# A fused attention and feed-forward kernel: q and k of the first four pairs loaded in longer packets and turned by TensorE

## The chip, the cores and the metric

The kernel runs on one core of one Trainium2 chip. The metric is the device time of one execution in microseconds (us). The core has five engines with their own instruction queues, which run in order and wait for one another on semaphores: TensorE (PE, with its weight loads shown apart as PEld), VectorE (DVE), ScalarE (ACT), GpSimd (POOL) and SyncE (SP). Sixteen DMA engines move data; SP, ACT and POOL issue the transfers. TensorE writes only PSUM, from which ACT and DVE copy.

## The reference, cut to what matters

```python
batch, n_heads, seq, head_dim = 8, 8, 576, 64
scores = scale * np.matmul(q, k.transpose(0, 1, 3, 2))
thresh = np.max(scores, axis=-1, keepdims=True) - tau
scores = np.where(scores >= thresh, scores, -1000000000.0)
scores = scores - np.max(scores, axis=-1, keepdims=True)
attn = np.exp(scores)
attn = attn / (np.sum(attn, axis=-1, keepdims=True) + 1e-09)
attn_out = np.matmul(attn, v)
x = attn_out.transpose(0, 2, 1, 3).reshape(B * S, H * D)      # 4608 x 512
h = x @ w_in                                                  # 512 x 2048, float64 input
g = h * (1.0 / (1.0 + np.exp(-1.702 * h)))
out = g @ w_out                                               # 2048 x 512, float64 input
```

The attention inputs are fp32. The two weight matrices come as 64-bit floats, and the kernel turns them into fp32 itself with integer and float steps on ACT and DVE.

## The kernel before

**Pairs.** The 64 heads are worked as 32 pairs of heads (pair n is two heads of batch n // 4). One pair goes through these steps, and each is a function in the code:

- `load_qk` (L392): q and k of one head, each as two DMAs of 32 columns. A packet is 32 floats, 128 bytes. A pair's q, or its k, is 2304 packets. The data lands in 32x32 blocks, ready for the next step.
- `prep` (L501): one DVE transpose of 32x32 blocks (L504) turns 128x576 of q, another those of k, so that the head dimension lies on the partitions.
- `scores` (L510, L514): for each of nine key blocks j, four matmuls of 64 partitions fill one PSUM tile of the pool psA (three tiles of two banks).
- `keep` (L527, L531): ACT copies that tile to SBUF.
- `in_groups` (L533, L537), `over_tiles`, `over_halves`: DVE reduces to the row maximum. For most pairs `turn_rows`, `row_out` (L630) and `row_in` (L639) send the maximum to DRAM and back, spread over the partitions; POOL issues that for pairs 0 to 7. Pair 2 spreads it on DVE instead (`spread_max`, L618).
- `sub` (L645, DVE), `mask` (L651, ACT) and `exps` (L655, ACT), five tiles a pair.
- `values` and `sums_by_pe` (L666): products with v, and with ones for the sums. For pairs 0 to 4 the sums are made on TensorE; later pairs reduce on DVE.
- `one_row` (L697), `spread_sums` (L749, L751), `place_x` (L768): DVE divides and writes x for the dense layers.

**Weights.** Each of 32 pieces of 512 KB is loaded by SP (`load_w`, L453) and converted in steps: `cv_power` (L461) and `cv_power2` (L465) on ACT, `cv_low` (L472) on DVE, `cv_round` on ACT for w_in (L479) or `cv_whole` on DVE for w_out (L486), and `cv_end` (L493) on DVE.

**Dense layers.** The first two blocks of 256 rows of x go through `mm1_0` (L823), `tanh`, `gelu_0` (L829) and `mm2` (L805) once pairs 0 to 3 are placed. Later blocks use seven products where eight would be needed (L783, L974 and, near the end, L888), with sums of weights that are made once by ACT, and by DMAs that add (L930, L934). `gelu` is L795.

**Order.** No engine picks work at run time. While the program is built, a planner (`run_in_order`) plays the tasks through, each with an engine, an estimated cost, a rank, the tasks it follows and the buffers it takes and gives back; of what is ready, an engine takes the lowest rank. Its choices become the fixed order of each queue. The rank of a pair's task is the pair's number plus a bias by function, from the tables `EARLY` (pairs 0 to 3), `SECOND` (4 to 7) and `LATER`; weight steps have `CV` and `W_RANK`. Loads of a pair have rank n - 2 plus the bias, v's own. Pairs 1 and 3 (`APART`) keep their raw, turned and score tiles in a second arena; the other pairs share one set of raw and turned tiles, so a load waits until its predecessor was turned.

```python
    def two_loads(n, which, cost, r, queue, behind, take):
        ys, a = [], None
        ring = RING[1] if queue is nc.sync else ()
        for h in range(2):
            a = task(
                "SP", cost, r, load_qk, n, which, queue, h,
                after=behind + ([a] if h else []), take=ring if h else tuple(take) + ring,
            )
```

Of the kernel before, what the change touches and what calls it, by code (L numbers as in the profile page):

```python
# [21 lines left out]
P = 128  # L22
# [10 lines left out]
def kernel(  # L33
# [84 lines left out]
    minus = const.tile([P, 2, KT], FP32, name="minus")  # L118
    own_row = const.tile([P, QB // 2], FP32, name="own_row")
# [10 lines left out]
    for x in ("raw0", "raw1", "qkT0", "qkT1", "mb"):  # L130
# [6 lines left out]
        "exps": 11.43,  # L137
        "in_groups": -31.63,
        "keep": -11.23,
        "load_qk": 20.14,  # L140
        "load_v": 19.9,
        "mask": 171.06,
        "one_row": -45.66,
        "over_halves": -1.59,
        "over_tiles": -20.68,
        "place_x": -28.05,
        "prep": -4.32,
        "row_in": 9.72,
        "row_out": -14.48,
        "scores_run": -28.58,  # L150
        "spread_max": 3.58,
        "spread_sums": 14.71,
        "sub": 178.85,
        "sums_by_pe": 312.21,
        "turn_rows": -14.38,
        "values": -19.56,
        "w_sum": -20.0,
    }
    SECOND = {
        "exps": 6.76,  # L160
        "in_groups": 291.18,
        "keep": 29.15,
        "load_qk": 165.77,
        "load_v": 335.03,
        "mask": 337.17,
        "one_row": -25.48,
        "over_halves": -20.33,
        "over_tiles": 311.35,
        "place_x": 0.09,
        "prep": -16.41,  # L170
        "row_in": 205.66,
        "row_out": 181.09,
        "scores_run": 21.47,
        "spread_sums": -6.66,
        "sub": 17.25,
        "sums_by_pe": 334.76,
        "sums_in": -21.09,
        "sums_out": 5.24,
        "turn_rows": 184.92,
        "turn_sums": -18.91,  # L180
        "values": -19.14,
    }
    LATER = {
        "exps": 208.23,
        "in_groups": 342.52,
        "keep": -7.99,
        "load_qk": 197.24,
        "load_v": -11.46,
        "mask": 344.07,
        "over_halves": -19.6,  # L190
        "over_tiles": 19.84,
        "place_x": 181.51,
        "prep": 208.92,
        "row_in": -6.54,
        "row_out": -30.86,
        "scores_run": -0.21,
        "sub": 200.03,
        "sums_in": 338.15,
        "sums_out": 7.27,
        "turn_rows": 167.17,  # L200
        "turn_sums": 343.8,
        "values": -25.3,
        "x_sum": -9.1,
# [1281 lines left out]
```

## Time and profile before

| | us |
|---|---|
| three runs: median (lowest to highest) | 1299.56 (1298.23 to 1299.97) |
| the profiled execution: its time | 1299.66 |
| its span | 1297.9 |
| PE busy | 1252.3 |
| DVE busy | 986.2 |
| ACT busy | 677.7 |
| first scores (L514) start | 9.06 |
| scores of pair 1 start | 21.41 |
| `mm1_0` (L823) starts | 108.59 |

The profile is one execution. The span runs from the first to the last instruction, and the execution's own time is 1.8 us longer. A row of the timeline gives the start, the duration, the engine, the line, what is written and read, the count, and in brackets the idle time of the engine just before and what ended it. Matmul counts of the profile are records: an fp32 matmul leaves two. The granted clock is the clock that TensorE was given, 1.00 being full.

### The profile page before, as it was taken

How to read it: one execution, taken by the hardware profiler on the slowest of the kernel's cores; microseconds unless marked ns; L12 is line 12 of the kernel's file. 1: busy time of each engine (PE TensorE's matmuls, PEld its weight loads, DVE VectorE, ACT ScalarE, POOL GpSimd, SP SyncE). 2: the span in 40 equal slices, each digit the busy share in tenths (PEclk: the TensorE clock that was granted, in tenths of full speed). 3: DMA queues.
4: the chain of work that ended last, by engine and by line, in shares of the span. 5: the costliest groups of instructions: out<-in, count | busy, mean ns of one | idle time of the engine just before them, and what ended most of it. 6: DMA issues, size and time to landing. Idle time of an engine off the chain costs nothing. (4 is left out here: it accounts for less than half of the span.)

```text
span 1297.9 us, 22745 instructions
## 1 busy us (share of the span) xinstructions
PE 1252.3 (96%) x9128; PEld 972.9 (75%) x9128; DVE 986.2 (76%) x1553; ACT 677.7 (52%) x878; POOL 240.6 (19%) x277
## 2 busy tenths in 40 slices
PE   4689999999999999999999999999999999999998
PEld 2347854577777888777777788887777788888887
DVE  6999987989988787777887878777778863652642
ACT  5999876686755545454555555544546540210210
POOL 1000101131030303021120312030302117120120
PEclk8799999999999999999999999999999999999999
DMA  9735356183222222222122222222221100000000
GB/s 243 179 76 146 109 132 115 58 144 84 72 55 56 56 72 56 72 47 64 55 48 63 47 63 56 72 56 73 55 61 35 51 27 17 1 1 33 1 1 33
DMA packets 190825, 87.01 MB, mean 67 GB/s; under 512 B 159872, under 2 KB 170112, under 8 KB 190720
## 3 DMA queue, kind: packets, MB, share of 16 engines
q1 hardware_dynamic: 182560, 78.08, 23.7%
q0 software_dynamic: 5792, 7.19, 3.1%
q8 instruction: 71, 1.16, 0.4%
q10 hardware_dynamic: 2368, 0.30, 0.2%
q14 instruction: 34, 0.28, 0.1%
HBM read 71.63 MB, written 9.70 MB: 63 GB/s over the span
## 5 line engine op out<-in xcount | busy, mean ns | idle before, releaser
L537 DVE TRANSPOSE_TENSOR_REDUCE part<-arena 128x36 f32<-128x1152 f32 (+1 forms) x295 | 358.1, 1236 | 48.1 <-ACT arena L531 38.2
L783 PE MATMUL hps<-xT,w_in 128*128 128x256 f32 x1536 | 338.9, 381 | 2.9 <-DVE arena L795 2.9
L783 PEld LDWEIGHTS hps<-xT,w_in 128*128 128x128 f32 x1536 | 291.8, 191 | 48.9 <-issue 5.3
L651 ACT ACTIVATE arena<-arena 128x1152 f32<-128x1152 f32 (+1 forms) x160 | 169.4, 1059 | 127.4 <-DVE arena L645 127.2
L531 ACT COPY arena<-ps 128x576 f32<-128x576 f32 x288 | 171.0, 642 | 111.8 <-PE ps L514 108.9
L645 DVE TENSOR_TENSOR arena<-arena 128x1152 f32<-128x1152 f32 (+1 forms) x158 | 202.1, 1320 | 19.2 <-DMA arena<-row 19.1
L974 PE MATMUL ops<-w_out,arena 128*128 128x256 f32 x896 | 202.7, 381 | 1.7 <-DVE arena L795 1.6
L655 ACT ACTIVATE arena<-arena,shift,scl 128x1152 f32<-128x1152 f32 (+1 forms) x160 | 200.1, 1250 | 4.0
L974 PEld LDWEIGHTS ops<-w_out,arena 128*128 128x128 f32 x896 | 169.1, 190 | 29.4 <-DVE arena L795 3.8
L514 PE MATMUL ps<-arena 64*64 64x288 f32 x2304 | 172.1, 413 | 19.5 <-DVE neg L1035 9.1
L940 POOL TENSOR_TENSOR arena<-arena 128x256 f32<-128x256 f32 x56 | 51.8, 925 | 647.1 <-DVE arena L795 544.0
L666 PE MATMUL pv<-arena 64*64 64x288 f32 x2176 | 159.6, 407 | 0.0
L974 PE MATMUL ops<-arena 128*128 128x256 f32 x672 | 150.6, 380 | 0.0
L792 ACT ACTIVATE th<-hps 128x512 f32<-128x512 f32 x112 | 66.1, 590 | 161.7 <-PE hps L783 148.2
L514 PEld LDWEIGHTS ps<-arena 64*64 64x64 f32 x2304 | 85.4, 135 | 81.5 <-ACT arena L531 17.5
L974 PEld LDWEIGHTS ops<-arena 128*128 128x128 f32 x672 | 127.3, 190 | 19.3 <-issue 2.2
L666 PEld LDWEIGHTS pv<-arena 64*64 64x64 f32 x2176 | 81.0, 133 | 54.7 <-issue 8.8
L996 DVE SCALAR_TENSOR_TENSOR osb<-ops,osb 128x256 f32<-128x256 f32 x98 | 39.6, 415 | 94.2 <-PE ops L974 88.0
L795 DVE SCALAR_TENSOR_TENSOR arena<-th,hps 128x512 f32<-128x512 f32 x96 | 64.3, 670 | 37.4 <-ACT th L792 37.0
L908 ACT ACTIVATE th<-arena 128x512 f32<-128x512 f32 x32 | 20.3, 635 | 72.6 <-DVE arena L904 72.6
L953 POOL TENSOR_TENSOR arena<-arena 128x512 f32<-128x512 f32 x28 | 37.4, 1340 | 106.7 <-PE ops L974 106.6
L805 PE MATMUL ops<-w_out,arena 128*128 128x512 f32 x128 | 56.8, 598 | 0.0
(118 smaller groups left out, 1072.8 us busy)
## 6 DMA issues: line engine op xcount, KB each, us to landing
arena<-in_v_dram SPq DMA_DIRECT2D x128, 144.0 KB
arena<-in_q_dram SPq DMA_DIRECT2D x128, 72.0 KB
out_dram<-osb SPq DMA_DIRECT2D x36, 256.0 KB
arena<-in_k_dram SPq DMA_DIRECT2D x124, 72.0 KB
arena<-row SPq DMA_DIRECT2D x48, 144.0 KB
arena<-row_s SPq DMA_DIRECT2D x48, 144.0 KB
w_out<-in_moe_w_in_dram SPq DMA_DIRECT2D x12, 512.0 KB
arena<-in_moe_w_out_dram SPq DMA_DIRECT2D x12, 512.0 KB
```

Source lines behind the costliest of these rows:

```text
L514: nc.tensor.matmul(ps[ts(c, KT), h, 0:SH], lhsT=mats[n, 1][ts(h, D), ts(j, KT)], rhs=mats[n, 0][ts(h, D), ts(c, SH)], start=True, stop=True,)
L531: nc.scalar.copy(out=sT[n, t][:, u], in_=pss.pop((n, j))[:, :, 0:SH])
L537: nc.vector.tensor_reduce(out=stats[n, op][:, t * 2 * QB : min(2 * t + 2, NK) * QB], in_=sT[n, t].rearrange("p u h (g d) -> p (u h g) d", ...
L645: engine.tensor_tensor(out=s, in0=s, in1=mbs[n].unsqueeze(1).to_broadcast(list(s.shape)), op=ALU.subtract)
L651: nc.scalar.activation(out=s, in_=s, func=AF.Prelu, alpha=STEEP)
L655: nc.scalar.activation(out=s, in_=s, func=AF.Exp, scale=scl, bias=shift)
L666: nc.tensor.matmul(o[c][ts(h, D), 0:SH], lhsT=left(j, h)[ts(c, KT)], rhs=sT[n, t][ts(c, KT), u, h, :], start=(j == 0), stop=(j == NK - 1),)
L783: nc.tensor.matmul(hidden[j][:, ts(f, BLK)], lhsT=w_in[:, c, ds((f * HF + j) * P, P)], rhs=xTs[blk][:, c, :], start=(c == 0), stop=(c == N ...
L792: nc.scalar.activation(out=ths[j], in_=hidden[j], func=AF.Tanh, scale=GELU_SCALE / 2)
L795: nc.vector.scalar_tensor_tensor(out=g[:, :, j, :], in0=two(ths.pop(j)), scalar=1.0, in1=two(hidden.pop(j)), op0=ALU.add, op1=ALU.mult,)
L805: nc.tensor.matmul(acc[i], lhsT=g0[:, j, ts(i, P)], rhs=w_out[:, j, :], start=(j == 0), stop=(j == NFC - 1),)
L974: nc.tensor.matmul(banks[blk][k][:, ts(o, HM)], lhsT=left[:, j, :], rhs=right[:, j, :], start=(j == 0), stop=(j == HF - 1),)
```

## The change

For pairs 0 to 3 (`TURNED`), `load_qk` loads k of a head as 64 rows of nine keys (2304 bytes a packet) in one DMA, and q in its natural rows of 64 floats (256 bytes a packet) in two DMAs, one for rows 0 to 511 and one for the last 64. TensorE turns both with a unit matrix (`turn_in`) into a PSUM tile of psA, and the result is copied to SBUF by ACT for q and by DVE for k (`turned`). The DVE transposes of these pairs go. The costs that the planner is given for these tasks follow, and its queue limits for SP (`RING`) get a fourth entry.

Each load of pairs 0 to 7 gets a rank of its own (`L_RANK`). All tables of biases and `W_RANK` are new, and with them the order of the queues throughout the kernel. Three buffers of `part` instead of two and four of `red` instead of two are allowed. `in_bank` and the changed lines about `TWICE` belong to a path that no pair takes (`TWICE` is empty), and two of the planner's costs for weight steps change.

```diff
+    eye = const.tile([P, P], FP32, name="eye")
     EARLY = {
-        "load_qk": 20.14,
-        "load_v": 19.9,
...
+        "load_qk": 43.19,
+        "load_v": -4.29,
...
+        "turn_in": 74.21,
...
+        "turned": 43.15,
...
     SECOND = {
-        "load_qk": 165.77,
...
+        "load_qk": 63.23,
...
     LATER = {
-        "load_qk": 197.24,
...
+        "load_qk": 0.86,
...
+    TURNED = (0, 1, 2, 3)
...
+        raws[n, which] = t
+        if n in TURNED:
+            rows = src[b, 2 * hp + h]
+            if which:
+                queue.dma_start(out=t[ts(h, D), :], in_=rows.rearrange("(k j) d -> k (j d)", k=KT))
+                return
+            queue.dma_start(
+                out=t[:, 0 : 4 * P].rearrange("p (c d) -> p c d", d=P)[:, :, ts(h, D)],
+                in_=rows[0 : 4 * P].rearrange("(c p) d -> p c d", p=P),
+            )
+            queue.dma_start(out=t[ts(h, D), 4 * P : S], in_=rows[4 * P : S])
+            return
...
+    def turn_in(n, which):
+        raw = raws.pop((n, which))
+        bank = pss[n, -1 - which] = psA.tile([P, 2, 512], FP32, name="ps", tag="ps")
+        ps = bank.rearrange("p a b -> p (a b)")
+        x = 0 if which else 4 * P
+        for o in range(0, x, P):
+            nc.tensor.transpose(ps[:, ds(o, P)], raw[:, ds(o, P)], eye)
+        for o in range(x, S, D):
+            for h in range(2):
+                nc.tensor.matmul(
+                    ps[ts(h, D), ds(o, D)], lhsT=raw[ts(h, D), ds(o, D)],
+                    rhs=eye[ts(h, D), ts(h, D)], start=True, stop=True,
+                )
+
+    def turned(n, which):
+
+        dst = home(n, f"qkT{which}")
+        ps = pss.pop((n, -1 - which)).rearrange("p a b -> p (a b)")[:, 0:S]
+        if which:
+            nc.vector.tensor_copy(out=dst, in_=ps)
+        else:
+            nc.scalar.copy(out=dst, in_=ps)
+        mats[n, which] = dst
...
-    W_RANK = (175.06, 5.72, 196.05, 310.62, 82.78, -16.51)
+    W_RANK = (2.76, 28.46, 63.86, 288.06, 13.26, 171.93)
...
+    L_RANK = (-36.61, -56.52, 96.67, 20.17, 8.58, 61.69, -10.29, 2.98, 30.6, 57.97, 57.07, 63.3, -5.89, 32.6, 22.95, 51.21, 10.58, 34.61, 280.62, 124.22, 93.66, 53.02, 2.42, 116.75)
...
-        lq = two_loads(n, 0, 1.15, r - 2.0, q0, behind, own(n, "raw0"))
-        lk = two_loads(n, 1, 1.15 if n else 0.05, r - 2.0, q1, behind, own(n, "raw1"))
+        lq = two_loads(n, 0, r - 2.0 + load_rank(n, 0), q0, behind, own(n, "raw0"))
+        lk = two_loads(n, 1, r - 2.0 + load_rank(n, 1), q1, behind, own(n, "raw1"))
...
+        if n in TURNED:
+            pq, pk = (
+                task("PE", (0.95, 1.0)[x], r, turn_in, n, x, after=y, take=("psA",), give=own(n, f"raw{x}"))
+                for x, y in enumerate((lq, lk))
+            )
+            pq = task("ACT", 0.56, r, turned, n, 0, after=[pq], take=own(n, "qkT0"), give=("psA",))
+            pk = task("DVE", 0.66, r, turned, n, 1, after=[pk], take=own(n, "qkT1"), give=("psA",))
+        else:
```

In the changed kernel's queues, SP's loads begin with q of pair 0, k of pair 1, a weight piece, q of pair 1, a weight piece, q and k of pair 2, two weight pieces, the first half of k of pair 3, and then v of pair 0; ACT issues k of pair 0. ACT's queue begins with the copy of q of pair 0, one weight step (L461), two score copies, a weight step and seven score copies. TensorE's begins with k and q of pair 0, k of pair 1, the scores of pair 0, and then q of pair 1, q and k of pair 2 and the scores of pair 1.

More of the change, by code (lines that the diff above doesn't have):

```diff
@@ L158 @@
+        "sums_by_pe": 64.77,
+        "turn_in": 74.21,
+        "turn_rows": 12.8,
+        "turned": 43.15,
+        "values": 190.42,
+        "w_sum": -9.84,
     }
     SECOND = {
[L160 to L171 removed]
@@ L172 @@
[L172 to L181, printed above, removed]
+        "exps": 24.5,
+        "in_groups": 172.55,
+        "keep": 18.55,
+        "load_qk": 63.23,
+        "load_v": -35.03,
+        "mask": 107.85,
+        "one_row": 71.99,
+        "over_halves": 396.59,
@@ L188 @@
[L188 to L203, printed above, removed]
+        "exps": 125.92,
+        "in_groups": 328.11,
+        "keep": -7.86,
@@ L1082 @@
         ]
-        m = task("ACT", 0.67, rank, cv_power, i, after=[a] + over)
+        m = task("ACT", 0.74, rank, cv_power, i, after=[a] + over)
         m = task("ACT", 0.65, rank, cv_power2, i, after=[m])
```

136 lines of the change are left out of this document (93 added, 43 removed).

## The prediction

> **What bounds the kernel now.** I read the page's busy shares first, then busy time by stretch, then TensorE's waits, then the start in order of time.
>
> ```profile
> PE 1252.3 (96%) x9128; PEld 972.9 (75%) x9128; DVE 986.2 (76%) x1553; ACT 677.7 (52%) x878; POOL 240.6 (19%) x277
> ```
>
> TensorE is idle for 1297.9 - 1252.3 = 45.6 us. The question is where.
>
> ```profile
> 0.00:20.00 20.00, 6.29 (x72) 2.96 (x72) 9.78 (x18) 8.57 (x14) 2.80 (x21) 0.98 0.88 196
> 20.00:40.00 20.00, 6.86 (x72) 3.65 (x72) 17.23 (x27) 16.35 (x26) 4.10 (x8) 0.67 1.04 295
> 40.00:60.00 20.00, 17.56 (x248) 10.69 (x248) 18.99 (x23) 18.68 (x23) 0.12 (x1) 0.84 0.59 160
> 60.00:80.00 20.00, 17.34 (x274) 9.48 (x272) 19.12 (x36) 19.83 (x24) 0.99 (x2) 1.00 0.50 97
> 80.00:100.00 20.00, 16.00 (x248) 8.72 (x248) 19.79 (x34) 19.80 (x24) 1.08 (x3) 1.00 0.31 70
> ```
>
> The columns are stretch, length, then busy time of PE, PEld, DVE, ACT and POOL, then the granted clock, the DMA share and GB/s. Until 40 us the DMA engines are full and ACT and DVE are not; from 40 to 100 us ACT and DVE are full and TensorE waits for them. Later it is the other way round: 161.4 of 161.4 us of TensorE are busy from 108.59 to 270, and 1003.3 of 1005 from 285 to 1290.
>
> ```profile
> 7.57 1.44 DVE L504 STREAM_TRANSPOSE arena<-arena 128x576 f32<-128x576 f32 x2 [7.57 <-DMA arena<-in_v_dram]
> 9.06 6.29 PE L514 MATMUL ps<-arena 64*64 64x288 f32 x72 [9.06 <-DVE neg L1035]
> 10.36 0.64 ACT L531 COPY arena<-ps 128x576 f32<-128x576 f32 x1 [8.12 <-PE ps L514]
> ...
> 21.41 6.86 PE L514 MATMUL ps<-arena 64*64 64x288 f32 x72 [6.07 <-DVE arena L504]
> ...
> 102.13 0.87 ACT L655 ACTIVATE arena<-arena,shift,scl 128x576 f32<-128x576 f32 x1
> ...
> 108.59 16.67 PE L823 MATMUL hps<-xT,w_in 128*128 128x256 f32 x76
> ```
>
> So the time is the hand-over at 108.59 (L823, the first dense product), plus a fixed length of TensorE work, plus 4.5 us of its later waits (0.64, 2.22, 0.83, 0.77) and a tail of 3.8. In the changed kernel's instruction order the same 216 score and 288 value and sum matmuls stand ahead of L823. What the change is worth is how far L823 moves. The chain to it: the last exponential of the fourth pair ends at 103.00, its values and `place_x` end at 107.40, L823 follows.
>
> **Part 1, the loads.** Four pairs of q and k are eight loads of 2304 packets of 128 bytes. In the first 9 us the ACT queue moved 2368 packets in 22.5% of 16 x 9 us, 13.7 ns each, so a load costs 2304 x 13.7 / 16 = 1.97 us of all sixteen engines, and eight cost 15.8 us of the full stretch. Changed, a k load is 128 packets of 2304 bytes. By bytes (295 KB) at the highest rate seen (331 GB/s, 24 to 28 us) that is 0.89 us. A q load is 1152 packets of 256 bytes: at least 0.89 by bytes, at most 1.97 if a packet of twice the size takes twice as long. I take 0.99, the same 13.7 ns a packet, as the short packets look bound by count: 2 to 6 us moved only 146 GB/s. Saved: 15.8 - 4 x 1.88 = 8.3 us, by the worst bound 4.3.
>
> The Trainium skill, "DMA: Bandwidth & Descriptors", Specifications, asks for 512 bytes and more and says that shorter transfers are read, modified and written; the 146 against 331 GB/s agrees. By it q at 256 bytes stays slow, and the saving would be nearer 4.3.
>
> **Part 2, the first pair.** q0 still takes SP four issues (0.75 to 3.09 us); with 1.9 us of data in place of 3.9 it lands at about 5.5 in place of 7.57. Then comes the new route. Turning q is 4 matmuls of 128 columns and 2 of 64: L823 runs 256 columns in 0.219 us a record, two records a matmul, so 0.22 each, about 1.0 in all. Turning k is 18 of 64 columns, two side by side, at the scores' pace (0.97 us for 16 records of 288 columns on four quadrants) also about 1.0, and k0 comes first. ACT's copy has L531's shape and source: 0.64. DVE's has no row: below, 0.64 as on ACT; above, 0.95 (L768, the same columns of PSUM in four pieces); I take 0.7, near L504's 0.74 for the same shape. Scores start near 7.5 in place of 9.06. The first copy of scores could follow at 8.8, but a weight step (L461) stands ahead of it on ACT and waits for the first weight piece: 5.5 + 0.9 (k1) + 1.8 (512 KB at 295 GB/s) = 8.2, plus 0.75. So the copies start at 9.0, not 10.36. Behind that waiting step stand all copies of pair 0, and TensorE and DVE behind them; it is the price of putting weights between pairs.
>
> **Part 3, ACT to the last exponential.** Up to 103.0 ACT is busy 86.2 us (1.5 of it the table) and idle 16.8: 8.9 before 10.36, 6.1 to 29, 1.4 to 55, 0.4 after. Work: 47 score copies, 40 masks and exponentials in both orders; 18 weight steps for 22 (-4 x 0.69 = -2.8) and four turned copies (+4 x 0.6 = +2.4): -0.4. Idle: pair 1's q and k now come ahead of weights and v, so its scores need not wait until 21.41. I expect 5.0 at the start (6.5 less the table's 1.5), 1.1 for the first weight piece, and a third of the old 7.9 us of gaps, 2.6: 8.7 in place of 16.8, a gain of 8.1 + 0.4 = 8.5. A second way is to walk ACT's changed queue with the trace's paces: a copy 0.56 in a row, a mask and exponential 2.44 together, 11.4 a pair, a weight step 0.7.
>
> - From 9.0, 26 copies of scores (14.6), three turned copies (1.9), 12 weight steps (8.4) and a pause of 1.0: pair 0's first mask at 34.9, in place of 39.0.
> - Pair 0: 46.3. Pair 1 with seven copies between: 60.8, and two more copies, 62.0. Pair 2 (69.9 now) with three copies: 75.2.
> - Five weight steps and nine copies: 84.2. Pair 3 with two copies: 96.9.
>
> The last exponential then comes 6.1 earlier. I take **7**, nearer the walk. DVE's subtractions for these masks come out at 33.5, 42.7, 55.1 and 81.6, each ahead of its mask; the last has the least cover, 2.6 us, and what is later than that is paid.
>
> DVE must follow: to `place_x` it is busy about 92 us. It loses 8 transposes (5.8), 7 L472 (4.4) and 2 L493 (1.3), and gains 4 copies (2.8) and three reductions with a small one (3.6): -5.1. To end at 100.4 it may idle 13.5 us, against 15.4 now and a start 2 us sooner. It holds, barely. POOL's row trip (out at 20.83, in by about 31.3, with 3.1 for the last landing) starts at 19.1 and is in at 29.6; the first subtraction comes at 32.2, so it stays hidden with 2.6 us of cover.
>
> **Part 4, after the hand-over.** The weight steps put off (4.4 + 1.3 = 5.7 us of DVE, 2.8 of ACT) fall into 100 to 160 us, where DVE idles 3.7 and ACT 4.2. The last w_out piece is ready at 179.86 and its product at 188.57 needs it: 8.7 us of cover now. In the changed order it stands behind three reductions after pair 4's `place_x`, and TensorE puts two products ahead of the values: I work out 1 us of cover. What is later than that is paid in full. Bounds: 0 and +3; I take 0. The later waits I keep at 4.5 (bounds 0 and 8). All other ranks are new as well, but the multiset of work on each engine is the same.
>
> **The sum.** The profiled execution took 1299.66 (span 1297.9), 0.1 above the median of 1299.56. 1299.66 - 7.0 = **1292.7**.
>
> **Rivals.**
> - *Given back at the weights.* L823 moves by 7, but the weight work put off holds TensorE for 3: 1295.7 to 1297. For: DVE and ACT are over 90% busy to 160. Against: from 108.59 to 270 DVE idles 17.3 us and ACT 36.6. Chance 0.17.
> - *The start stays put.* The new route is longer (1.0 + 0.64 and two hand-overs, against 0.74 a transpose), three PSUM buffers are shared by turned matrices and scores, and only the 1.4 us of the first copy remain: 1298.3. For: ACT and DVE are full from 29 us on. Against: ACT's 6.1 us gap. Chance 0.12. The Trainium skill, "VectorE: DVE Perf Modes", Rules for kernel authors, calls the DVE transpose the fastest within 32x32 blocks; it speaks for this rival, and no run yet shows TensorE's.
> - *Slower.* In the later pairs two transposes (L504) stand straight ahead of a gelu (L795) on DVE in both orders. Before 275.17 one waits 3.33 us for a k load, TensorE stands 2.22 us, and the granted clock falls to 0.81 and 0.76 for 8 us (about 1.8 more): 4 us a time. With all later ranks redone, from three such stalls on (12 > 7 + 2.6) the kernel is slower: 1304.7. For: every rank changes. Against: q and k loads get lower ranks in both later groups (165.77 to 63.23, 197.24 to 0.86; lower goes first), and now only 1.6 us are lost after 285. Chance 0.10.
>
> The forecast (1287 to 1295) has 0.61, which includes a gain of 8.5 with the stall at 277 gone. A difference of 0.2%, 2.6 us, is about what a measurement of this kernel can tell from no change. Faster by more: 0.61 + most of the first rival = 0.76; within: 0.14; slower: 0.10. The range 1286.5 to 1299 takes in the forecast and two rivals and leaves out the slower one.
>
> **What would show it.** In the profile after: first scores near 7.5 us; the first score copy near 9; pair 1's scores before 17; DMA full for less than 40 us; ACT idle to the last exponential of pair 3 near 9 us; L823 near 101.6; TensorE without a new gap from there to 270. I am wrong if L823 stays above 106, if DVE's copy from PSUM takes over 1 us, or if TensorE's idle time after L823 exceeds 8 us.

## The result, and the profile after

The changed kernel took **1306.5 us** (median of 8 runs, beside 1299.7 for the kernel before on the same chip): ratio 1.0042, 95% interval 1.0027 to 1.0058. A second series of the same kernel gave 1304.81 (1303.63 to 1306.85) and again 1.0042 (1.0028 to 1.0055). I had forecast 1292.7 and a range up to 1299.0, so the result is outside it and on the other side. The execution profiled in the first series ran at a lower granted clock throughout (0.915, 1374.4 us; the ratio leaves it out), so the profile after, here and below, is that of the second series (it took 1304.03, span 1302.3).

The busy shares come first, then busy time by stretch, in the columns of before:

```profile
PE 1262.7 (97%) x9304; PEld 981.9 (75%) x9304; DVE 983.3 (76%) x1549; ACT 673.2 (52%) x882; POOL 240.2 (18%) x279
```

```profile
0.00:20.00 20.00, 14.58 (x216) 10.23 (x217) 9.79 (x16) 10.96 (x19) 3.22 (x23) 1.00 0.82 222
20.00:40.00 20.00, 10.76 (x172) 5.21 (x172) 14.90 (x25) 15.44 (x28) 3.15 (x6) 0.89 1.01 278
40.00:60.00 20.00, 16.78 (x240) 9.80 (x244) 19.57 (x30) 19.76 (x20) 1.06 (x2) 0.86 0.45 86
60.00:80.00 20.00, 15.28 (x222) 9.56 (x216) 19.09 (x31) 17.03 (x20) 1.86 (x4) 0.91 0.12 33
80.00:100.00 20.00, 16.15 (x232) 9.32 (x228) 18.14 (x27) 19.83 (x26) 0.23 (x1) 0.91 0.83 202
```

Until 20 us every engine but VectorE (9.79 us for 9.78) does more than before: ACT 10.96 us for 8.57. From 20 to 40 ACT and DVE are less busy than before, and from 60 to 80 ACT is again, although work waits for them (ACT 15.44 for 16.35 and 17.03 for 19.83). So the lead was made and then lost, at two places. The DMA engines are nearly as full until 40 us as they were (0.82 and 1.01 for 0.88 and 1.04). By then both kernels have asked for twelve pieces of weights, and the changed one has moved all of q and k of the four pairs, the one before six and a half of its eight loads. The slack came later, at 40 to 60 us (0.45 for 0.59) and at 60 to 80 (0.12 for 0.50).

The first dense product (L823, now L873) starts at 107.93, only **0.66 us** earlier where I had forecast 7.0. TensorE's later waits, the span after L873 less its busy time (1181.3 us, 1181.1 before) and the tail of 3.7, are **9.4 us for 4.5**. Rows of TensorE's timeline behind L873 that begin with a wait:

```profile
150.76 7.51 PE L873 MATMUL hps<-xT,w_in 128*128 128x256 f32 x32 [1.12 <-DVE arena L879]
158.82 7.17 PE L873 MATMUL hps<-xT,w_in 128*128 128x256 f32 x32 [0.55 <-DVE arena L879]
...
270.45 3.72 PE L833 MATMUL hps<-xT,w_in 128*128 128x256 f32 x16 [0.37 <-DVE arena L845]
278.36 11.83 PE L833 MATMUL hps<-xT,w_in 128*128 128x256 f32 x47 [4.19 <-DVE arena L845]
```

Two more stand at 348.96 (0.74; one of 0.83 before) and at 1083.77 (2.16, again behind a gelu, L845). The sum is 1299.66 - 0.66 + 4.9 + 0.2 = 1304.1, against the 1304.03 of this execution. It has to close, as the waits are what is left over of the span; what it shows is that TensorE's busy time behind L873 is the same in both.

**Where the lead was lost.** Three views of the kernel after show it. GpSimd's timeline, with pair 0's row of maxima going out (L680) and coming in (L689):

```profile
22.19 1.08 POOL L680 DMA_DIRECT2D row<-flat  x2 [18.08 <-DVE flat L629]
29.66 1.06 POOL L689 DMA_DIRECT2D arena<-row  x2 [6.40 <-DMA row<-flat]
```

VectorE's, with the first subtraction that needs this row:

```profile
38.60 3.90 DVE L695 TENSOR_TENSOR arena<-arena 128x1152 f32<-128x1152 f32 x3 [4.54 <-DMA arena<-row]
```

And ScalarE's: its last weight step ahead of the first mask, then the mask.

```profile
35.00 0.84 ACT L475 ACTIVATE w_in<-arena,rebias 128x512 f32<-128x512 int16 x1
39.99 1.16 ACT L701 ACTIVATE arena<-arena 128x1152 f32<-128x1152 f32 x1 [4.15 <-DVE arena L695]
```

ScalarE was ready at 35.84, close to the 34.9 of my walk, and stood 4.15 us for a row that took 16.4 us from 22.19 to 38.60; I had given the trip 10.5. That was too little for the kernel before as well. Its two transfers back, in GpSimd's timeline, and their median time from issue to landing, in the DMA view from 27 to 34 us:

```profile
26.71 0.54 POOL L639 DMA_DIRECT2D arena<-row  x1 [4.80 <-DMA row<-flat]
27.63 0.53 POOL L639 DMA_DIRECT2D arena<-row  x1 [0.38 <-DMA row<-flat]
```

```profile
arena<-row POOLq DMA_DIRECT2D x2, 144.0 KB, 6.0
```

So the row was in at 33.6, and the trip took 12.8 us from 20.83. My 3.1 us for the last landing is the median over all transfers of this kind that GpSimd issues in the kernel. In the kernel after, the two took 5.4 and 8.3 us and the row was in at 38.5: the trip grew by 3.5 us, not by 5.9. The second place is pair 1's `place_x` on VectorE, with TensorE and ScalarE behind it:

```profile
65.47 3.89 DVE L575 TRANSPOSE_TENSOR_REDUCE part<-arena 128x36 f32<-128x1152 f32 x3
...
71.51 0.95 DVE L818 TENSOR_TENSOR xT<-pv,arena 128x256 f32<-128x256 f32 x4
```

```profile
72.61 0.86 PE L552 MATMUL ps<-arena 64*64 64x288 f32 x8 [4.34 <-DVE xT L818]
```

```profile
73.51 0.64 ACT L569 COPY arena<-ps 128x576 f32<-128x576 f32 x1 [2.80 <-PE ps L552]
```

`place_x` empties a PSUM tile of psA. Three reductions of pair 3's scores (3.89 us) stand ahead of the sums and `place_x`, so TensorE can't make pair 3's next scores for 4.34 us, and ScalarE has nothing to copy for 2.80.

### The profile page after: what moved, and what is told of

It is laid out like the page before. It is cut to its first block, busy times and chain, and to the rows that moved or that the text cites. A ratio compares the mean times of both kernels' runs of the same rounds, so it can differ in the third digit from the quotient of the medians.

```text
span 1372.6 us, 23092 instructions
## 1 busy us (share of the span) xinstructions
PE 1344.7 (98%) x9304; PEld 1006.2 (73%) x9304; DVE 989.1 (72%) x1549; ACT 676.7 (49%) x882; POOL 240.2 (18%) x279
## 5 line engine op out<-in xcount | busy, mean ns | idle before, releaser
L833 PE MATMUL hps<-xT,w_in 128*128 128x256 f32 x1536 | 356.4, 396 | 1.5 <-DVE arena L845 1.5
L833 PEld LDWEIGHTS hps<-xT,w_in 128*128 128x128 f32 x1536 | 296.2, 194 | 60.7 <-issue 6.2
L701 ACT ACTIVATE arena<-arena 128x1152 f32<-128x1152 f32 (+1 forms) x160 | 165.7, 1059 | 136.3 <-DVE arena L695 135.7
L1024 PE MATMUL ops<-w_out,arena 128*128 128x256 f32 x896 | 211.8, 394 | 1.3 <-DVE arena L845 1.3
L705 ACT ACTIVATE arena<-arena,shift,scl 128x1152 f32<-128x1152 f32 (+1 forms) x160 | 194.6, 1244 | 1.8
L552 PE MATMUL ps<-arena 64*64 64x288 f32 x2304 | 182.1, 433 | 5.6 <-DVE xT L818 3.6
L716 PE MATMUL pv<-arena 64*64 64x288 f32 x2176 | 171.1, 432 | 0.0
L1024 PE MATMUL ops<-arena 128*128 128x256 f32 x672 | 157.9, 393 | 0.0
L552 PEld LDWEIGHTS ps<-arena 64*64 64x64 f32 x2304 | 89.0, 138 | 72.7 <-ACT arena L569 11.4
L845 DVE SCALAR_TENSOR_TENSOR arena<-th,hps 128x512 f32<-128x512 f32 x96 | 64.7, 673 | 53.6 <-ACT th L842 53.2
L855 PE MATMUL ops<-w_out,arena 128*128 128x512 f32 x128 | 66.0, 677 | 0.0
L873 PE MATMUL hps<-xT,w_in 128*128 128x256 f32 x256 | 64.4, 422 | 0.0
L873 PEld LDWEIGHTS hps<-xT,w_in 128*128 128x128 f32 x256 | 50.5, 198 | 13.9 <-issue 0.5
```

Of the source, the lines that this page charges most:

```text
L552: nc.tensor.matmul(ps[ts(c, KT), h, 0:SH], lhsT=mats[n, 1][ts(h, D), ts(j, KT)], rhs=mats[n, 0][ts(h, D), ts(c, SH)], start=True, stop=True,)
L701: nc.scalar.activation(out=s, in_=s, func=AF.Prelu, alpha=STEEP)
L705: nc.scalar.activation(out=s, in_=s, func=AF.Exp, scale=scl, bias=shift)
L716: nc.tensor.matmul(o[c][ts(h, D), 0:SH], lhsT=left(j, h)[ts(c, KT)], rhs=sT[n, t][ts(c, KT), u, h, :], start=(j == 0), stop=(j == NK - 1),)
L833: nc.tensor.matmul(hidden[j][:, ts(f, BLK)], lhsT=w_in[:, c, ds((f * HF + j) * P, P)], rhs=xTs[blk][:, c, :], start=(c == 0), stop=(c == N ...
L873: nc.tensor.matmul(hidden[j][:, ts(i, BLK)], lhsT=w_in[:, c, ts(j, P)], rhs=xTs[i][:, c, :], start=(c == 0), stop=(c == NDC - 1),)
```

## The experiments

The kernels in one table. L873 is its start, "waits" are TensorE's behind it, worked out as above, "busy" is TensorE's busy time behind it.

| kernel | median us (runs) | ratio to before, 95% | first copy | first mask | L873 | waits | busy |
|---|---|---|---|---|---|---|---|
| before | 1299.7 (8) |  | 10.36 | 39.00 | 108.59 | 4.5 | 1181.1 |
| after_again | 1304.81 (5) | 1.0042 (1.0028-1.0055) | 11.86 | 39.99 | 107.93 | 9.4 | 1181.3 |
| turned_only | 1311.88 (4) | 1.0095 (1.0081-1.0109) | 9.83 | 41.82 | 114.13 | 9.2 | 1183.3 |
| spread0 | 1304.33 (8) | 1.0027 (1.0017-1.0037) | 10.41 | 31.62 | 105.09 | 7.1 | 1184.3 |
| places6 | 1311.27 (5) | 1.0084 (1.0071-1.0096) | 10.36 | 35.80 | 104.14 | 14.8 | 1185.1 |
| places8 | 1308.91 (5) | 1.0065 (1.0051-1.0079) | 11.87 | 37.73 | 106.78 | 12.9 | 1186.3 |
| places10 | 1311.87 (4) | 1.0091 (1.0077-1.0104) | 11.44 | 38.78 | 107.28 | 14.2 | 1184.1 |
| late_old | 1314.84 (4) | 1.0107 (1.0091-1.0122) | 11.01 | 39.33 | 111.66 | 13.4 | 1185.2 |
| spread0_late | 1310.66 (5) | 1.0075 (1.0063-1.0088) | 10.92 | 31.30 | 109.26 | 11.7 | 1185.6 |
| behind_gelu | 1301.94 (11) | 1.0007 (0.9998-1.0016) | 11.24 | 38.82 | 107.95 | 7.1 | 1182.2 |
| row0_dve | 1304.45 (10) | 1.0031 (1.0022-1.0039) | 10.60 | 36.21 | 106.26 | 8.9 | 1184.2 |
| place1_early | 1303.92 (11) | 1.0013 (1.0002-1.0024) | 11.15 | 39.84 | 106.49 | 9.6 | 1182.7 |
| all_three | 1305.26 (10) | 1.0027 (1.0014-1.0040) | 11.50 | 35.50 | 103.98 | 14.5 | 1182.7 |
| late_fixed | 1300.70 (11) | 0.9998 (0.9988-1.0007) | 12.40 | 40.03 | 108.90 | 6.6 | 1180.9 |
| all_fixed | 1295.20 (5) | **0.9958 (0.9944-0.9971)** | 10.81 | 34.82 | 102.38 | 6.1 | 1180.9 |

"First copy" is ScalarE's first copy of scores. In kernels with the same instructions up to there (after_again, behind_gelu and the last five) it lies between 10.60 and 12.40 from one execution to another, so single profiles differ by up to 2 us at the start. Where L873 of two kernels is compared below, I take it from the first copy on: 96.1 us in after_again, 98.2 before. Three kernels have the same instructions up to L873, and they give 96.1 (after_again), 96.7 (behind_gelu) and 96.5 (late_fixed); from the first copy to the first mask it is 28.1, 27.6 and 27.6, and 28.7 in place1_early, which has the same instructions so far. Differences of about 0.6 us at L873 and 1 us at the mask are therefore not told apart by single profiles.

### after_again: the changed kernel once more

No edit.

> The changed kernel once more, for an undisturbed profile and its granted clock. Theory A (the row trip): the maximum of pair 0 goes through DRAM on DMA engines that SP keeps full with weight pieces, so pair 0's first mask starts near 39.0 as before, and the first dense product (L873) near 108 to 111; TensorE's idle time after it stays under 6 us. Theory B (the clock): the hand-over comes early, below 105, and the loss lies in a lower granted clock after it: the mean clock from the hand-over to the end is under 0.99 where the kernel before has 1.00. Time about 1302 to 1308 by both.

The first mask and L873 came as theory A had them (39.99; 107.93, just under its 108), but behind L873 TensorE waited 9.4 us where A had less than 6. B falls for this profile: the clock behind the hand-over is 1.00 in both kernels, and 0.89 from 270 to 285 in both. A explains the start only. For the rest there was a third theory, C of the next run: the new ranks of the later pairs cost.

The profile doesn't speak for every execution. Of the twelve that count in the two series, five had a mean granted clock of 0.992, as the profiled one, and took 1301.87 to 1304.88 us; seven had 0.986 to 0.989 and took 1304.81 to 1307.75. The executions of the kernel before that are on record with their clock all had 0.990 to 0.992. So a lower clock goes with some 3 us in more than half of the executions, and B may hold a part of the median. No trace shows where these seven lost it.

### turned_only: the new loads and turns with the old ranks

```diff
 EARLY, SECOND, LATER, CV, W_RANK and two costs of weight steps as before; turn_in, turned: rank of prep
-    L_RANK = (-36.61, -56.52, ...)
+    L_RANK = ()
```

> The changed loads and the turning by TensorE with all ranks of the kernel before (no rank for each load). Theory A: the loads themselves do help at the start (first scores 1 to 2 us sooner), and what spoils it is the order of weight pieces around the trip; with the old ranks twelve weight pieces stand together behind the loads, ahead of the trip, so the first mask is not sooner than 37 and the time is 1297 to 1303. Theory B: the turning work on TensorE is what lowers the clock, so the clock after the hand-over is as low as in the changed kernel and the time is over 1302. A third theory (C: the new ranks of the later pairs cost): the time falls to 1294 to 1298, as the later ranks are the old ones.

1311.88: none of the three holds. A's mask was right (41.82, not sooner than 37) and B's time (over 1302), but not A's time (to 1303) nor B's clock (1.00 behind the hand-over), and C is far off. Old ranks on the new tasks make a poor order: on ScalarE six weight steps run in a row from 87.89 to 91.84, and TensorE waits 5.25 us until then. Its L873 comes at 114.13. This run can't price the turns alone: order and tasks go together.

### spread0: no trip for pair 0, replanned

```diff
-    BY_DMA = (0, 1, *range(3, NP))
+    BY_DMA = (1, *range(3, NP))
```

> The changed kernel, but pair 0's row of maxima is spread by VectorE (as pair 2's is) and makes no trip through DRAM. Theory A (the trip of pair 0's row through DMA engines that are full until 40 us ate the earlier start): with no trip the first subtraction and the first mask come at 32 to 35 us in place of 39.99, the first dense product (L873) at 102 to 105 in place of 107.93, and the kernel takes 1299 to 1302. Rival D (ScalarE and VectorE are full from there on and a later queue sets the hand-over, whatever the first mask does): the first mask comes earlier all the same, but L873 stays at 107 or later and the time at 1304 to 1306.

The mask came at 31.62, and L873 94.7 us after the first copy, 1.4 us sooner than as changed: the trip did cost. But only 0.5 us shows in the median (the ratio is 1.0027 for 1.0042, with intervals that overlap), so that the time is D's, while L873 is just past A's bound of 105. The planner made another order from the edit (five weight steps that stood ahead of the first mask went behind pair 0's last), so what was lost again can't be read from it.

### places6, places8, places10: fewer weight pieces in flight while the row travels

```diff
-            every = HALVES[:4] + W64[:2] + HALVES[4:] + W64[2:]
+            every = HALVES[:4] + W64[:2]                  # places6
+            every = HALVES[:4] + W64[:2] + HALVES[4:6]    # places8
+            every = HALVES[:4] + W64[:2] + HALVES[4:]     # places10
```

> The changed kernel with six staging places for the pieces of w_in in place of twelve, so that the later pieces are asked for only as places come free; no instruction of the row's trip is changed. Theory A (the trip is slow because twelve pieces of weights and pair 4's q and k keep the DMA engines full until after 33 us): the DMA share falls below 1 before 30 us, the trip from the row's first issue to the first subtraction takes 10 to 12 us in place of 16.4, the first mask comes at 34 to 36. L873 then comes up to 4 us earlier unless the late pieces hold the weight steps. Rival E (the trip is slow for a reason of its own, the queues of POOL and SP or the place of the issues in their order): it still takes 15 to 17 us, and the first mask stays at 39 to 41.

> The changed kernel with eight staging places for the pieces of w_in (six gave the mask of pair 0 at 35.80 and L873 at 104.14, but 18 us of later waits; twelve, as changed, 39.99, 107.93 and 9.3). If the row's trip is slowed by the weight pieces asked for while it runs, taking four of them out of that time should do most of what six places did: first mask at 35.8 to 37.5, L873 at 104 to 106, and fewer late pieces than with six places: later waits of 8 to 14, time 1299 to 1306. If it is the number of q and k packets instead, which the planner now sends in that time, the mask comes at 38 or later.

> The same with ten places: only the last two of twelve pieces wait. By the weight pieces (1 MB, about 3.5 us of the full DMA at 290 GB/s, taken out of the time of the trip): the first mask between those of eight and twelve places, 37 to 39, L873 at 105 to 107, later waits 7 to 11, time 1299 to 1305. If the loss at the start is something other than these pieces, 39.5 to 40.5 and 107 to 108.5.

GpSimd's timeline of places6 shows the same two steps of the row as above:

```profile
20.93 1.07 POOL L680 DMA_DIRECT2D row<-flat  x2 [16.83 <-DVE flat L629]
25.21 0.54 POOL L689 DMA_DIRECT2D arena<-row  x1 [3.22 <-DMA row<-flat]
```

With six places the row is on its way back 4.3 us after it went out, in place of 7.5, and the mask no longer waits for it. From the first issue to the last landing the trip takes 11.5 us with six places, 12.0 with eight, 13.4 with ten, and 15.4 to 16.9 in the four traces with twelve and the same order (16.3 in after_again). From the first copy to the mask it is 25.4, 25.9, 27.3 and 28.1 us; to L873 it is 93.8, 94.9, 95.8 and 96.1, of which the step from twelve to ten lies within the spread above. So each step that takes pieces out of the trip's time shortens it: E is refuted. A is right that the pieces are the cause, but not in its reason: it had the DMA share fall below 1 before 30 us, and with six places it is 1.24 from 25 to 33 us. Eight places missed their bounds by 0.2 us at the mask and 0.8 at L873, and ten places by 0.3 at L873, which is in the other theory's range there. The price is on the other side: pieces that come late hold TensorE later (4.13 us behind a weight step, L507, in places6). The waits are 13 to 15 us (14.8 with six places; the 18 in the expectation for eight include the tail), and all three kernels are slower, by more than I expected of eight and ten.

**Load or length of packets?** The DMA views while pair 0's row comes in, of the kernel after (30 to 38 us) and of places6 (25 to 33 us). In order: packets and MB, the share of the sixteen engines by queue (q1 carries SP's transfers, q0 GpSimd's), and the row's time from issue to landing in the last column.

```profile
DMA packets 608, 2.05 MB, mean 257 GB/s; under 512 B 120, under 2 KB 120, under 8 KB 606
...
q1 hardware_dynamic: 510, 1.73, 75.8%
q0 software_dynamic: 96, 0.30, 17.4%
...
arena<-row POOLq DMA_DIRECT2D x2, 144.0 KB, 6.9
```

```profile
DMA packets 4590, 1.61 MB, mean 202 GB/s; under 512 B 4239, under 2 KB 4239, under 8 KB 4588
...
q1 hardware_dynamic: 4460, 1.29, 99.8%
q0 software_dynamic: 128, 0.30, 22.0%
...
arena<-row POOLq DMA_DIRECT2D x2, 144.0 KB, 5.2
```

places6 has the fuller engines, and its row still lands sooner. What differs is the mean packet: 3.4 KB as changed, 0.35 KB there. In the kernel before it is 1.2 KB at this step (27 to 34 us, also full) and the landing 6.0. So it is not fullness alone: the row's packets seem to wait longer behind long ones. The Trainium skill, "DMA: Bandwidth & Descriptors", Queues, rings and completion order, says that an engine goes round its queues packet by packet and finishes a packet before it turns to the next queue. The order of the three landings agrees, though a packet in the skill is a bundle of descriptors, and the view's packets need not be the same unit. No run here varied the length alone, so this is argued and not shown.

### late_old, spread0_late: the old ranks for the later pairs

```diff
 SECOND, LATER as before      # spread0_late: BY_DMA as in spread0, too
```

> The changed kernel with the ranks of the later pairs as they were before the change (tables SECOND and LATER); first pairs, weights and loads ranked as changed. Theory C (the new ranks of the later pairs cost about 5 us behind the hand-over): TensorE's waits after L873 fall from 9.3 to 4 to 6, L873 stays within 2 us of 107.93, and the kernel takes 1299 to 1302. Rival F (those waits come from the weight steps and loads that the first pairs put off, whatever the later ranks): they stay at 8 or more, and the time at 1303 to 1307.

> Both edits together: pair 0's row spread by VectorE, and the ranks of the later pairs as they were before the change. If A and C both hold and add up: L873 at 102 to 105, waits behind it 4 to 6, and 1294 to 1298, faster than the kernel before. If the two losses are one (the order behind the hand-over only takes what the start gives): 1299 to 1302. If D and F hold: 1304 or more.

C is refuted as put: with the old tables the waits rise to 13.4, L873 moves to 111.66, and the two kernels are 10 and 6 us slower than after_again and spread0. The new tables are better for the new start than the old ones. I took the loss to lie in particular places of the new order, not in the tables as a whole, and went on with edits that keep the planner's order and move single instructions.

### behind_gelu: three places of VectorE's order

```diff
-                tasks[i][3](*tasks[i][4])
+                emit(tasks, i)    # holds the tasks named here until the gelu behind them is in the queue:
+BEHIND = {sub of pair 4, tile 0: next gelu_0; prep of pair 10, k: next gelu; x_sum 14 (four): gelu 7}
```

> The changed kernel with three places of VectorE's order edited and all else the same, instruction for instruction: the first subtraction of pair 4 (it waits 2.68 us for its row), the second transpose of pair 10 (it waits 5.21 us for k) and four sums of x (5 us of work behind a late place_x) each go behind the gelu that stood after them. Theory G (the extra waits after L873 are gelus held by a VectorE instruction ahead of them that waits for a DMA): TensorE's waits after L873 fall from 9.3 to 1 to 4 us, L873 stays at 107.9, and the kernel takes 1297 to 1300. Rival H (TensorE is short of VectorE's and ScalarE's work there, so that the wait moves to the next gelu or to the scores that follow): the waits stay at 7 or more and the time at 1303 to 1306.

1301.94, 2.9 us below after_again, with L873 at 107.95 and waits of 7.1: G holds at two places and not at the third; the time lies between G's range and H's, and the waits are at H's bound. The wait at 1083 is gone, and those near 150 fell from 1.67 to 0.92. Around 280 us it only moved from one gelu to the next:

```profile
281.30 2.93 PE L833 MATMUL hps<-xT,w_in 128*128 128x256 f32 x6 [4.55 <-DVE arena L845]
```

VectorE's timeline there, same kernel, shows what else stands ahead of that gelu: two DMAs, and subtractions behind the second.

```profile
276.22 0.78 DVE L518 STREAM_TRANSPOSE arena<-arena 128x576 f32<-128x576 f32 x1 [4.76 <-DMA arena<-in_k_dram]
278.02 2.63 DVE L695 TENSOR_TENSOR arena<-arena 128x1152 f32<-128x1152 f32 x2 [1.02 <-DMA arena<-row]
280.57 0.68 DVE L845 SCALAR_TENSOR_TENSOR arena<-th,hps 128x512 f32<-128x512 f32 x1
```

### row0_dve, place1_early: the two places of the start, one by one

```diff
     def turn_rows(n):
+        if n == 0: return spread_max(n)      # row0_dve; row_out and row_in do nothing for pair 0
...
+BEHIND = {in_groups of pair 3, tiles 0 to 2: place_x of pair 1}    # place1_early
```

> The changed kernel with pair 0's row spread by VectorE and nothing else moved: the four DMAs of its trip are gone from GpSimd, five small instructions of VectorE are replaced by six at the same place, and TensorE, ScalarE and SyncE keep their orders instruction for instruction. Theory A: ScalarE had its weight steps done at 35.84 and waited 4.15 us for the row, so the first mask comes at 36 to 36.5; L873 comes 3 to 4 us earlier than 107.93 (104 to 105) and the later waits stay at 8 to 10, so 1300.5 to 1302.5. Rival D (a wait further on takes it back): the mask at 36 but L873 at 107 or later and 1304 to 1305.

> The changed kernel with one edit of VectorE's order: three reductions of pair 3's scores go behind the sums and place_x of pair 1, which hold one of the three PSUM buffers. Theory P (TensorE's wait of 4.3 to 5.2 us at 72 for that buffer, and ScalarE's of 2.8 to 4.1 behind it, are a second part of the loss at the start): the wait falls below 1.5 us, pair 3's first mask comes 2 to 4 us earlier than 89.81 and L873 at 104 to 106; 1301 to 1303. Rival Q (the reductions put off are needed as soon as place_x, so the wait only moves to pair 3's row): pair 3's first mask within 1 us of 89.8, L873 at 107 to 108.5, 1304 to 1306.

In row0_dve ScalarE goes from its weight step straight to the mask, as A had it:

```profile
35.55 0.83 ACT L475 ACTIVATE w_in<-arena,rebias 128x512 f32<-128x512 int16 x1
36.21 1.23 ACT L701 ACTIVATE arena<-arena 128x1152 f32<-128x1152 f32 x1
```

From the first copy to the mask it is 25.6 us in place of 28.1, but to L873 95.7 in place of 96.1: of 2.5 us at most 0.4 is left, which is within the spread, because the second place takes the rest. TensorE of row0_dve, then of place1_early:

```profile
70.65 1.24 PE L552 MATMUL ps<-arena 64*64 64x288 f32 x8 [5.84 <-DVE xT L818]
```

```profile
69.28 0.72 PE L552 MATMUL ps<-arena 64*64 64x288 f32 x8 [1.05 <-DVE xT L818]
```

The wait for `place_x` grew from 4.34 to 5.84 in the one and fell to 1.05 in the other, where pair 3's first mask came at 87.22 (89.81 as changed). From the first copy on that is 1.9 us sooner, but L873 only 0.7 (95.3), hardly more than the spread. It lies between P's bounds and Q's, as row0_dve's lies between A's and D's. Alone, each edit leaves the other wait, which takes most of the gain (in place1_early the first mask still waits 4.74 us for the row). In the time, row0_dve gives nothing that can be measured, and place1_early moves the ratio from 1.0042 to 1.0013, more than its profile (1304.35, near its slowest) shows. Both left the stall at 276 to 278 us (4.79 and 4.70 us for 4.19).

### all_three: both, and the later places

The edits above, with the transpose of pair 10's k put behind two gelus and the five subtractions of pair 9 behind three.

> Both edits above, and the gelus of behind_gelu (whose waits behind L873 were 7.0 in place of 9.3, and 1301.9) with its second place mended: the transpose of k and the five subtractions of pair 9, which wait for DMAs until 278, go behind two and three gelus. If A, P and G each hold and the parts add: first mask near 36, L873 at 101 to 103, later waits 2 to 5, 1292 to 1296, faster than the kernel before by 0.3 to 0.6%. If A and P repair the same wait twice, L873 at 104 and 1295 to 1298. If what comes early only waits longer at the next late DMA, later waits of 7 or more and 1299 or more.

At the start the two edits are worth 3.6 us together (L873 92.5 us behind the first copy), where they were worth 0.4 and 0.7 alone. Behind it the waits are 14.5. By its new place the transpose came behind the load of pair 11's k into the same tile, so it waited 12.02 us for that, and pair 10's scores of this kernel are made with pair 11's k. Its time says nothing on the theories.

### late_fixed, all_fixed: the same with the load kept behind the transpose

```diff
+BEHIND adds: load_qk of pair 11, k: prep of pair 10, k
 late_fixed: only the later places; all_fixed: with row0_dve and place1_early
```

> The changed kernel with only the later places of VectorE's order edited: as in behind_gelu, but around 270 us the transpose of k goes behind two gelus and the five subtractions of pair 9 behind three (and the load of pair 11's k is issued behind that transpose, since it writes where the transpose reads). Theory G: the waits behind L873 fall from 9.3 (7.0 in behind_gelu, 4.55 of them at 281) to 1.5 to 4, L873 stays at 107.9, and 1296 to 1299.5. Rival H: TensorE needs the transposed k or the masks of pair 9 soon after, so 3 us or more are lost again between 275 and 300, and the time is 1300 to 1303.

> The same, with pair 0's row spread by VectorE and place_x of pair 1 ahead of three reductions: the start as in all_three (first mask 35.50, L873 103.98, 3.95 us earlier than as changed), and the later order of late_fixed. If what comes early at L873 stays gained: 3 to 4 us below late_fixed, 1292.5 to 1296, faster than the kernel before. If the transfers of the time from 250 to 285 keep their own times whatever L873 does, the earlier start is waited away at 275 to 300: within 1.5 us of late_fixed, later waits larger by 2.5 to 4.

late_fixed is at 0.9998 of the kernel before: the later places of VectorE's order are worth 4.1 us of the changed kernel, in the median; its profile shows 2.8 of them as waits. These are still 6.6, more than G had, and the time is in H's range and not in G's. One wait of 4.06 us stays at 288.76, now behind five subtractions that run without a break (7.42 us). H is right at this one place, though it was this edit that put the five together; spreading them between gelus wasn't tried. all_fixed is 5.5 us below late_fixed (its L873 comes 91.6 us after the first copy, for 96.5), and **0.42% faster than the kernel before** (0.29 to 0.56). So in this pair of kernels an earlier L873 stays gained. Its start is the one that I had walked through: first mask 34.82 (34.9 predicted), pair 3's first mask 84.33 (84.2), L873 102.38 (101.6). In part that is luck: its first copy came at 10.81 where the walk began at 9.0, and pair 0's row makes no trip in it.

```profile
20.00:40.00 20.00, 12.76 (x188) 6.37 (x192) 19.70 (x27) 19.24 (x31) 1.38 (x3) 0.92 1.01 277
...
60.00:80.00 20.00, 17.86 (x279) 10.42 (x271) 19.06 (x35) 19.83 (x26) 2.07 (x4) 1.00 0.27 61
```

ACT's busy time in the two stretches where the lead was lost is now 19.24 (15.44 as changed) and 19.83 (17.03), with the DMA engines as full as ever until 40 us.

## Why the prediction was wrong, point by point

- **What bounds the kernel** was right: the start of L873, a fixed length of TensorE work (1181.1 and 1181.3 us) and the later waits make up the time. The waits are worked out as the rest, so this sum closes for every kernel in the table; what could have failed is the fixed length, and it is up to 5 us longer in some. Two of my three signs of being wrong came: L873 above 106 (107.93), and more than 8 us of waits behind it (9.4).
- **Part 1, the loads.** "Saved: 8.3 us" was mis-sized: by the packet records of the two traces it is 4.9, near the worst bound of 4.3. The eight loads took 15.5 us of the sixteen engines before; as changed the four of q took 6.0 (20.6 ns a packet of 256 bytes, where I had taken 13.7) and the four of k about 4.6 (145 ns a packet of 2304 bytes, those of v among them). And the saving was beside the point. The DMA engines stayed full until 40 us, as the twelve weight pieces are asked for by 32 us. What a transfer loses was not priced: the row trip runs through those same engines.
- **Part 2, the first pair.** The copies out of PSUM were right (0.76 us on DVE for 0.7 predicted, 0.64 on ACT). The turn of k was not: "about 1.0" against 2.18 and 2.29 us for the first two, 1.3 later. I priced 18 matmuls by the scores' pace and left out that each turns another tile, so that weight loads fill it: PEld was busy 1.99 of the 2.18 us, and 1.13 of 1.26 later. That is 0.3 us of the miss. The rest falls only on the first two, in a stretch where the scores of the kernel before ran at half their later pace, too (last section). The first weight piece landed at 9.57 (8.2). Scores start at 10.44 (7.5; 9.06 before) and the first copy comes at 11.86 (9.0; 10.36 before). Of these 2.9 us only 0.9 is left where ScalarE is ready for the first mask (35.84 for 34.9), since my walk had allowed for more idle time on the way.
- **Part 3, the step that failed.** "So it stays hidden with 2.6 us of cover": I moved an old trip of 10.5 us by the earlier start, to be in at 29.6. It was in at 38.5, and ScalarE waited 4.15 us. Of these 8.9 us, 3.1 are the later start (22.19 for 19.1), 2.3 are my reading of the old trip (12.8, so that the cover was 0.3 us and not 2.6), and 3.5 are what the trip grew by beside the new traffic. The first two alone would have put the row in at 35.0 and the first mask near 36.3, about 0.5 us behind ScalarE's steps. "It holds, barely" was the second: I added up VectorE's busy time to `place_x` of the last pair, but not what `place_x` of pair 1 stands behind; 2.80 us of ScalarE. row0_dve, place1_early and all_three show both: mending one alone brings 0.4 to 0.7 us, hardly more than the spread of single profiles, and both 3.6 (4.9 from late_fixed to all_fixed).
- **Part 4.** The last w_out piece cost nothing, as taken. "The later waits I keep at 4.5 (bounds 0 and 8)": 9.4. The new order has VectorE wait for a late row, a late k and a late sum ahead of gelus. behind_gelu and late_fixed show 2.3 to 2.8 us of the 4.9 more than before; the stall near 280 us stays in every version of this order, at 4.1 to 4.8 us (2.2 before; all_three apart).
- **The rivals.** "The start stays put" (0.12) had the place of L873 within 0.8 us, by causes of which one held: the longer route, and the three PSUM buffers, though not the turned matrices held them but `place_x`. I had set against it that ScalarE's gap of 6.1 us would close. It closed (its longest wait from 12 to 35 us is 0.41), and others opened. "Slower" (0.10) had the mechanism, a VectorE instruction that waits for a DMA ahead of a gelu, and its price of 4 us; but there is one such stall near 280 us, with smaller ones at 150 and 1083, not three of 4 us. The result is both rivals at once, which I had not allowed for: 1298.3 + 4.9 = 1303.2.
- **Left open**: why the stall near 280 us is longer than the 2.2 us of before. The transposes of pair 10's q and k stand side by side there, where before a reduction and a gelu stand between them; behind_gelu puts a gelu between them again, and the stall only moves. VectorE gets k 5.5 us after its last issue before and 7.9 us as changed, and nothing here shows why. A kernel with an earlier load of k wasn't tried. Open, too, is why the row's trip is longer behind the weight pieces: the length of packets is argued only.

## What to carry to other kernels

When transfers are freed, ask what the queue sends in their place: a small, late transfer that another engine waits for pays for the traffic beside it, and the price has to be read in the landing times of that very transfer, not in a median over the kernel, and not moved along with the start. In this kernel, whose orders are fixed when it is built, the lead survived only once instructions that wait on a DMA, or hold a scarce buffer, stood behind the work that others need sooner; such places are found by the timeline of the engine that is busy, and moving some fifteen instructions and sparing one trip was worth 9.6 us here, where the change as a whole had lost 5.

## What the runs showed of the hardware

- A turn of 128x576 fp32 by TensorE in 64x64 tiles (36 records) took about 2.2 us for the first two (34 records in 2.18; 37 in 2.29, four of them the end of q's turn) and 1.26 to 1.32 later; in 128x128 tiles the four matmuls took 1.11 us first and 0.66 later. The profile's rows give a granted clock of 1.00 there, but the trace holds no clock record before 11.6 us (12.2 in the kernel before), and a stretch without one counts as 1.00. The pace says otherwise. In the kernel before, eight records of scores start every 0.96 to 1.01 us from 9.06 to 12 us, the same as from 21.4 to 25.3 us, where the rows give 0.50 (20 to 24 us); after each of these stretches, at 1.00, it is 0.48 to 0.54 us. So the first 12 us probably ran at half the clock.
- Around the stall near 280 us the granted clock falls, and for different times after nearly the same stall. Slices of 4 us, the clock third from the end: kernel after, then place1_early.

```profile
276.00:280.00 4.00, 1.64 (x4) 1.37 (x5) 2.74 (x3) 2.13 (x3) 1.46 (x2) 0.73 0.95 133
280.00:284.00 4.00, 4.00 (x18) 3.40 (x17) 4.00 (x5) 0.47 (x1) 4.00 (x3) 0.84 0.35 53
```

```profile
276.00:280.00 4.00, 2.71 (x6) 2.19 (x7) 3.69 (x4) 0.55 (x1) 2.53 (x3) 0.58 0.73 95
280.00:284.00 4.00, 4.00 (x12) 3.22 (x11) 4.00 (x4) 0.00 (x0) 3.22 (x2) 0.56 0.19 28
```

The clock lost, as the sum of (1 - clock) x 4 us (some of it while TensorE still stands): 1.7 us in the first, 3.4 in the second (the traces have it at 0.50 for 3.4 and for 6.8 us). It is 1.7 in before, late_fixed and all_fixed too, and 3.4 in behind_gelu and row0_dve. The Trainium skill, "TensorE: Matmul & The Clock Gate", Part 1, says that the clock is halved after about 3.4 us of idle TensorE, and that the window in which idleness is counted runs freely, so that the same kernel can pay differently. Stalls of 4.1 to 4.8 us and two sizes of loss agree with it. The kernel before does not: a stall of 2.22 us cost it 1.7 as well, and in row0_dve one of 2.34 us at 1082.89 lowered the clock, while one of 2.16 at 1083.77 in after_again did not. So less than 3.4 us can be enough here.

The mean granted clock of each execution is on record. In row0_dve and place1_early it goes with the time: 1304.84, 1306.63 and 1306.84 us at 0.988 and 1301.25 at 0.992 in the one, 1304.62 and 1304.86 at 0.989 and 1298.08 to 1301.05 at 0.992 and 0.993 in the other. In behind_gelu and late_fixed, whose executions lie 5 us apart, too, it does not (1298.50 at 0.990 and 1303.42 at 0.991; 1296.98 and 1301.97, both at 0.989). So the clock is part of the spread in two of these kernels, and what else spreads them stays open.
